# Attention, an expert layer and a squared-ReLU layer on one core: where the float64 weights are narrowed, where operand differences are cast, which engine squares, and the order of units at stage borders

## The chip, the core and the metric

The kernel runs on one core of a Trainium2 chip. Times are device microseconds (us) of one execution. A core has a matrix engine (TensorE, PE in the profile), a vector engine (VectorE, DVE), a scalar engine (ScalarE, ACT), a general engine (GpSimd, POOL) and a queue engine (SyncE, SP) that issues all the transfers spoken of here. Each engine works through its own instructions in order and waits where an operand or a buffer is not ready.

## The reference

```
x = attention(q, k, v)                       # windowed, 8 heads, 4 x 576 tokens -> x: 2304 x 512
P = balanced gate of x @ w_gate              # 2304 x 8
for e in range(8):                           # expert layer, F = 1024
    out += P[:, e:e+1] * (np.maximum(x @ w1[e], 0) @ w2[e])
h = out @ w_in                               # 512 x 2048, drawn as float64
r = np.maximum(h, 0.0)
return (r * r) @ w_out                       # 2048 x 512, drawn as float64
```

## The kernel before

All products are done in float32 precision: each operand is cut into a high and a low part of the rounded matrix type, and a product is three matmuls (high x high, high x low, low x high). After the attention (until about 100 us) the work is 80 **steps** of one block of hidden columns each. Steps 0 to 31 run the expert layer over the first two 512-token halves and a single block of 256 tokens, steps 32 to 63 run it over the other two halves with weights that were kept in DRAM in split form, steps 64 to 71 and 72 to 79 run the squared-ReLU layer over the same two sets of tokens.

A step's first layer is done by seven products instead of eight, the units u1 to u7 (L591, banks s, pt, xt), from a weight block `blk` and sums of its parts `sum`. The second layer of the step before stands between them. In steps 1 to 20 and 65 to 72 it is plain units (`l2_units`, L816, three banks mm in a ring), added up by DVE (L842, scaled by the gate, or L846). In steps 21 to 64 and 73 to 79 it is seven products too, v1 to v7 (L912, `l2_mixed`), whose operands are differences of the hidden blocks; they are made ready a step earlier, from `TURN` = 20 on. `us` and w0, w1 belong to the single 256 tokens. A unit is six matmuls of 128x512 that start some 0.227 us apart, 1.36 us in all.

The order of everything is written by hand. A list `order` gives the units of a step; `after(k, f)` places work k units later, and what is placed at the same unit goes to the engines' queues in the order of the calls. `run(u)` writes a unit and what has come due.

- `prep_w` (from L162) says after which unit each weight is cast: high parts by ACT (`hi`, L172), low parts by DVE (`lo`, L176), sums and mixes of weight parts by POOL (m1 to m4), then stores to DRAM (L139) and, for kept weights, fetches (L143), both by SP. `load_w` (L158) loads the next raw weights into raw1 and raw2.
- `narrow` (L277) turns a piece of w_in or w_out, 512 KB of float64 seen as pairs of int32, into float32. It has a load and three stages of two, two and three DVE instructions (L289 and L293, L297 and L300, L304, L307 and L311), and stores the piece in `w32`. There are 32 pieces. `narrow_on` advances the sequence by a load or a stage. In steps 2 to 20 it is called after the units of the table `early`; where a piece ends, the next load follows at once, into a buffer of the pair xb. Three pieces fall into steps 52 to 61 and five into steps 64 to 69.
- `out_mixed` (from L675) makes the operands of v1 to v7. After u7, POOL makes four differences (L702), ACT casts their high parts (`operand`, L670) and DVE their low parts (L673).
- `unit` of `l2_mixed` copies v1's two banks to two other banks (L916, ACT), as v2 adds to the same product in place of the first.
- `evac_g` (from L612) squares the hidden block in the plain steps 64 to 71 (and for the single block): ACT makes the ReLU (L638), DVE the square (L642), ACT casts its high part (L648), DVE the low part (L628).
- At the end of the loop over steps stand the special orders of step 20 (`TURN`), 31, 32 (`NS1`) and 64 (`first[2]`).

Of the kernel before, what the change touches and what calls it, by code (L numbers as in the profile page):

```python
# [44 lines left out]
NWARM = 9  # L45
TURN = 20


@with_exitstack
def tile_kernel(ctx: ExitStack, tc: tile.TileContext, a):  # L50
# [70 lines left out]
    kept_back = []  # L121
    mixes, apart = [], []

# [27 lines left out]
    def load_w(i, which):  # L151
        if i >= len(steps) or kept(i):
            return
        moe, s = steps[i]
        while not moe and done[0] < 16 * s + 8 * which + 8:
# [8 lines left out]
    def prep_w(i, layers=(1, 2)):  # L164
# [55 lines left out]
        if kept(i):  # L220
            w2 = wset[i % 2]["w2"]
            out += [(0, lambda: fetch("w2", i, w2))]
            if mixed(i):
                out += [(5 if i == NS1 else 0, lambda: fetch("mix", i, mixes[i % 2]))]
            if i == 2 * NS1 - 3:
                out += [(2, lambda: load_w(2 * NS1 + 1, 0)), (2, lambda: load_w(2 * NS1, 1))]
        elif i >= 0:
            w2 = wset[i % 2]["w2"]
            moe = i < TURN
            r = raw2.rearrange("p (f e d) -> p f e d", f=FC, e=2)  # L230
# [45 lines left out]

    def narrow(which, s, k):  # L277

        n = 512
        src = (apart[0] if apart else xb()).bitcast(I32).rearrange("p (n w) -> p n w", w=2)  # L280
        cols = slice(2 * n * k, 2 * n * k + 2 * n)
        nc.sync.dma_start(
            src.rearrange("p n w -> p (n w)"), a["w_in" if which == 0 else "w_out"][s].bitcast(I32)[:, cols]
        )
        yield
        low, high = src[:, :, 0], src[:, :, 1]
        topf = apart[1] if apart else xb()[:, :n]
        top = topf.bitcast(I32)
        nc.vector.tensor_scalar(  # L289
            out=top, in0=high, scalar1=3, scalar2=0x3FFFFFFF,  # L290
            op0=ALU.logical_shift_left, op1=ALU.bitwise_and,
        )
        nc.vector.scalar_tensor_tensor(  # L293
            out=top, in0=high, scalar=-0x40000000, in1=top, op0=ALU.bitwise_and, op1=ALU.bitwise_or
        )
        yield
        nc.vector.tensor_scalar(  # L297
            out=high, in0=high, scalar1=0x7FFFFFFF, scalar2=None, op0=ALU.bitwise_and
        )
        nc.vector.scalar_tensor_tensor(  # L300
            out=topf, in0=high, scalar=float(0x38100000), in1=topf, op0=ALU.is_ge, op1=ALU.mult
        )
        yield
        nc.vector.tensor_scalar(  # L304
            out=high, in0=top, scalar1=-0x800000, scalar2=None, op0=ALU.bitwise_and
        )
        nc.vector.scalar_tensor_tensor(  # L307
            out=low.bitcast(F32), in0=low.bitcast(U32), scalar=2.0**-52, in1=high.bitcast(F32),
            op0=ALU.mult, op1=ALU.mult,
        )  # L310
        nc.vector.tensor_tensor(out=topf, in0=topf, in1=low.bitcast(F32), op=ALU.add)  # L311
        nc.sync.dma_start(w32[which, s, :, n * k:n * k + n], topf)
        yield

# [302 lines left out]
    def evac_g(i, ghi, glo, src, k):  # L617

        moe, s = steps[i]
        n = src.shape[-1]  # L620

        def low(z, relu):
            if relu:
                nc.vector.scalar_tensor_tensor(
                    out=glo, in0=z, scalar=0.0, in1=ghi.bitcast(F32), op0=ALU.max, op1=ALU.subtract
                )
            else:
                nc.vector.tensor_tensor(out=glo, in0=z, in1=ghi.bitcast(F32), op=ALU.subtract)  # L628
# [7 lines left out]
        def square():  # L636
# [3 lines left out]
        def product():  # L640
            held["g"] = tmp("g")[:, :n]
            nc.vector.scalar_tensor_tensor(  # L642
                out=held["g"], in0=src, scalar=0.0, in1=held["r"], op0=ALU.max, op1=ALU.mult
            )

        after(k, square)
        after(k + 1, product)
        after(k + 2, lambda: nc.scalar.copy(ghi, held["g"]))  # L648
        after(k + 3, lambda: low(held["g"], False))

    def l1_pair(i):
# [24 lines left out]
        def out_mixed(fc, t, src, k):  # L676
# [22 lines left out]
            elif (fc, t) == (1, 0):  # L699
                operand("21", g, k + 1, k + 2 if moe else k + 3)  # L700
            else:
                sub = lambda o, x, y: nc.gpsimd.tensor_tensor(out=o, in0=x, in1=y, op=ALU.subtract)  # L702

                def mix():
                    sub(r1, r4, r1)
                    sub(r5, r2, r1)
                    sub(r4, r2, r4)
                    sub(r3, r3, r5)

                after(2, mix)  # L710
                a, b, c, d = (4, 5, 7, 8) if i >= NS1 else (7, 6, 9, 11)
                operand("t1", r1, 3, a)
                operand("t2", r5, 4, b)
                operand("t3", r4, 5, c)
                operand("t4", r3, 6, d)

# [179 lines left out]
    def l2_mixed(i):  # L896
# [5 lines left out]
        whole = lambda f, e: [z[:, f, e] for z in w2]  # L902
        places = range(4) if steps[i][0] and steps[i][1] < TURN else (3, 0, 1, 2)
        mixed_w = lambda k: [z[:, places[k]] for z in mix]
# [46 lines left out]
    with tc.manual_schedule():  # L951
# [217 lines left out]

        narrows = (x for s in range(NS2) for which in range(2) for k in range(2) for x in narrow(which, s, k))  # L1170

        done = [0]

        def narrow_on():
            done[0] += 1
            next(narrows, None)

        def settled(i):

            while done[0] % 4:  # L1180
                narrow_on()

        for i in range(len(steps) + 1):
# [23 lines left out]
            if mixed(i - 1):  # L1207
# [12 lines left out]
                if i == first[1] - 1:  # L1220
                    names = "u1 v1 u2 v2 w0 u3 u4 v6 w1 u5 v5 u6 u7 v7 v3 v4 us"
# [18 lines left out]
            if i + 2 in first[1:]:  # L1240
                settled(i)
            if i + 1 in first[1:]:
# [22 lines left out]
            stages = {}  # L1265
            if 2 * NS1 - 12 <= i <= 2 * NS1 - 3:
                stages = ({8: 3, 9: 0} if i < 2 * NS1 - 3 else {8: 3}, {8: 1}, {8: 2})[(i - 2 * NS1 + 12) % 3]
            elif 2 * NS1 <= i <= 2 * NS1 + 5:
                stages = {2: 1, 4: 2, 6: 3, 8: 0}
            early = ()  # L1270
            if i == SCALED - 1:
                early = (2, 15, 16, 17)
            elif SCALED <= i <= TURN:
                early = ((1, 3, 5, 12), (1, 3, 10, 12), (1, 8, 10, 12) if i < TURN else (1,))[i % 3]
            for k, u in enumerate(order):
                run(u)
                if i < SCALED:
                    next(sink, None)
                if stages and done[0] % 4 == stages.get(k):
                    narrow_on()  # L1280
                if k in early:
                    narrow_on()
                    if done[0] % 4 == 0 and i < TURN:
                        narrow_on()
        settle()
# [86 lines left out]
```

## Time and profile before

| | us |
|---|---|
| median of 3 runs (1938.05 to 1941.02) | 1938.65 |
| the profiled execution, its own time | 1940.36 |
| its span in the trace | 1938.6 |
| PE busy in it | 1893.0 |
| DVE busy | 1663.1 |
| ACT busy | 791.5 |
| POOL busy | 660.6 |

The span is cut by the steps. In the trace u1 of step 3 begins at 161.71 us, that of step 20 at 634.86 (behind the layer-2 units of step 19, which begin at 617.50), step 21 begins at 649.25, step 31 at 905.05, step 32 at 932.23, step 64 at 1548.24 and step 65 at 1572.52. Plain steps of the first half take 26 to 27 us, mixed steps some 25 to 26 us. The granted TensorE clock is at its upper level nearly throughout (mean 0.998).

### The profile page before, as it was taken

To read this page: it belongs to the slowest core of one execution; us is meant where nothing else is said; L and a number is where in the kernel's file an instruction comes from. 1 tells how busy PE (TensorE), PEld (TensorE's weight loads), DVE (VectorE), ACT (ScalarE), POOL (GpSimd) and SP (SyncE) were. 2 spreads that over 40 slices of the span, in tenths; PEclk is the share of its full clock that TensorE was granted. 3 is DMA by queue.
4 is the path that set the end of the run, shared out by engine and by line. 5 is a ranking of instruction groups with operands and counts; after the bars stand their busy time and mean duration, and the time that the engine had idled before them with its cause. 6 is when DMAs were issued, how large, how long until landed. Compare 5 with 4: busy or idle time off the path is not lost.

```text
span 1938.6 us, 28282 instructions
## 1 busy us (share of the span) xinstructions
PE 1893.0 (98%) x10343; PEld 1561.4 (81%) x10343; DVE 1663.1 (86%) x2468; ACT 791.5 (41%) x1310; POOL 660.6 (34%) x584
## 2 busy tenths in 40 slices
PE   8998999999999999999999999999999999999999
PEld 6777888888888788888788888888888777888887
DVE  6787888888888798888789998999999989885897
ACT  6753332333332444444333333343333354443443
POOL 3532333332332344444323333332323334331231
PEclk9999999999999999999999999999999999999999
DMA  8686676776766556656967767676667777879661
GB/s 299 202 311 214 240 272 245 252 285 244 278 253 212 210 204 217 212 205 236 408 244 286 268 242 283 240 273 230 245 232 272 308 270 265 291 285 388 232 246 71
DMA packets 162555, 492.75 MB, mean 254 GB/s; under 512 B 16929, under 2 KB 32177, under 8 KB 162417
## 3 DMA queue, kind: packets, MB, share of 16 engines
q1 hardware_dynamic: 162416, 490.96, 69.4%
q8 instruction: 81, 1.33, 0.3%
q14 instruction: 58, 0.47, 0.1%
HBM read 282.15 MB, written 208.74 MB: 253 GB/s over the span
## 4 chain that ended last, share of the span: by engine, by line
PE 46%; DVE 8%; issue 1%; POOL 1%; ACT 0%; DVEq 0%; ACTq 0%; POOLq 0%
PE mm L912 11%; PE pt L591 9%; PE s L591 6%; PE xt L591 6%; PE mm L816 5%; PE s L912 4%; PE xt L912 4%; DVE acc L926 1%; PE mm L773 1%; DVE g L673 1%; POOL r L702 1%; DVE g L642 1%; DVE acc L846 0%; DVE mixl L176 0%; DVE mix L691 0%
## 5 line engine op out<-in xcount | busy, mean ns | idle before, releaser
L816 PE MATMUL mm<-w2h,g 128*128 128x512 f32 x928 | 289.1, 393 | 1.9 <-DVE acc L846 1.1
L702 POOL TENSOR_TENSOR r<-mix,r 128x512 f32<-128x512 f32 x51 | 67.4, 1321 | 597.6 <-DVE mix L691 510.1
L673 DVE TENSOR_TENSOR g<-r,g 128x512 fp32r<-128x512 f32 x204 | 197.6, 970 | 63.2 <-ACT g L670 61.5
L670 ACT CAST g<-r 128x512 fp32r<-128x512 f32 x204 | 126.5, 621 | 251.2 <-DVE r L691 111.7
L816 PEld LDWEIGHTS mm<-w2h,g 128*128 128x128 f32 x928 | 172.1, 188 | 40.9 <-DVE acc L846 4.7
L926 DVE TENSOR_TENSOR acc<-mm,acc 128x512 f32<-128x512 f32 x298 | 191.4, 679 | 8.1 <-PE mm L912 8.1
L842 DVE SCALAR_TENSOR_TENSOR acc<-mm,ptile,acc 128x512 f32<-128x512 f32 x194 | 142.4, 745 | 45.8 <-PE mm L816 45.5
L816 PE MATMUL mm<-w2l,g 128*128 128x512 f32 x464 | 180.8, 390 | 0.0
L912 PE MATMUL mm<-g,w2h 128*128 128x512 f32 x408 | 127.3, 393 | 9.7 <-ACT s L916 9.7
L190 POOL TENSOR_TENSOR sums<-raw 128x256 f32<-128x256 f32 x40 | 31.3, 782 | 295.2 <-DVE suml L176 213.9
L670 ACT CAST g<-mix 128x512 fp32r<-128x512 f32 x153 | 94.6, 620 | 86.3 <-POOL mix L702 75.6
L591 PE MATMUL xt<-x_hi,sumh 128*128 128x512 f32 x316 | 123.7, 391 | 2.4 <-DVE s L743 2.4
L912 PE MATMUL mm<-g,mixh 128*128 128x512 f32 x408 | 125.7, 389 | 0.0
L591 PE MATMUL s<-x_hi,blkh 128*128 128x512 f32 x316 | 123.5, 391 | 1.1 <-ACT pt L726 1.1
L591 PE MATMUL pt<-x_hi,sumh 128*128 128x512 f32 x316 | 123.3, 390 | 0.7 <-ACT s L738 0.7
L591 PE MATMUL s<-x_lo,blkh 128*128 128x512 f32 x316 | 123.1, 390 | 0.0
L591 PE MATMUL xt<-x_hi,suml 128*128 128x512 f32 x316 | 123.0, 389 | 0.0
L591 PE MATMUL s<-x_hi,blkl 128*128 128x512 f32 x316 | 123.0, 389 | 0.0
L591 PE MATMUL xt<-x_lo,sumh 128*128 128x512 f32 x316 | 123.0, 389 | 0.0
L591 PE MATMUL pt<-x_lo,sumh 128*128 128x512 f32 x316 | 123.0, 389 | 0.0
L591 PE MATMUL pt<-x_hi,suml 128*128 128x512 f32 x316 | 123.0, 389 | 0.0
L773 PE MATMUL mm<-xs,blkh 128*128 128x256 f32 x624 | 112.9, 280 | 1.9 <-DVE pT L562 1.2
(264 smaller groups left out, 4923.4 us busy)
## 6 DMA issues: line engine op xcount, KB each, us to landing
raw<-in_w SPq DMA_DIRECT2D x61, 512.0 KB, 4.8
blkh<-w_blkh SPq DMA_DIRECT2D x41, 512.0 KB, 3.7
blkl<-w_blkl SPq DMA_DIRECT2D x41, 512.0 KB, 4.5
sumh<-w_sumh SPq DMA_DIRECT2D x41, 512.0 KB, 5.3
suml<-w_suml SPq DMA_DIRECT2D x41, 512.0 KB, 6.1
w_blkh<-blkh SPq DMA_DIRECT2D x40, 512.0 KB, 5.3
w_blkl<-blkl SPq DMA_DIRECT2D x40, 512.0 KB, 6.4
w_sumh<-sumh SPq DMA_DIRECT2D x40, 512.0 KB, 5.6
```

The costliest lines, as they stand in the source:

```text
L190: tt(out=c(sums, 0), in0=c(raw1, 2), in1=c(raw1, 3), op=ALU.add)
L591: nc.tensor.matmul(ps, w[:, c], z[:, x, j], start=start and k == 0, stop=stop and k == 5, skip_group_check=True)
L642: nc.vector.scalar_tensor_tensor(out=held["g"], in0=src, scalar=0.0, in1=held["r"], op0=ALU.max, op1=ALU.mult)
L670: after(k, lambda: nc.scalar.copy(b[:, 0], src))
L673: lambda: nc.vector.tensor_tensor(out=b[:, 1], in0=src, in1=b[:, 0].bitcast(F32), op=ALU.subtract),
L702: sub = lambda o, x, y: nc.gpsimd.tensor_tensor(out=o, in0=x, in1=y, op=ALU.subtract)
L773: nc.tensor.matmul(ps, w[:, c], z[:, kc], start=k == 0, stop=k == len(terms) - 1)
L816: nc.tensor.matmul(ps, g[:, c0 * 128:c0 * 128 + 128], wt[:, fc], start=k == 0, stop=k == 3 * FC - 1)
L842: nc.vector.scalar_tensor_tensor(out=dst, in0=ps, scalar=p, in1=dst, op0=ALU.mult, op1=ALU.add)
L912: nc.tensor.matmul(ps, w[wt][:, c], z[:, g], start=start and k == 0, stop=stop and k == 2, skip_group_check=True)
L926: nc.vector.tensor_tensor(out=o, in0=ps, in1=o, op=ALU.add)
```

## The change

Line numbers after the change are some 29 to 31 higher from `narrow` on (L912 becomes L941, L916 L945, L670 L699, L842 L871, L591 L622).

**Narrowing.** `narrow` no longer loads; `load_raw` does, one or two pieces ahead. For the first 22 pieces (`DEEP`) raw data goes by turns into one xb buffer and into `mix32`, and the other xb buffer holds both scratch halves. The table of places becomes the same for every step from 3 to 19. As `mix32` is taken, the mixes of second-layer weights are made in place in raw2 from step 3 on (m3, m4 instead of m1, m2), and casts of w2 and of the mixes move.

```diff
-                early = (2, 15, 16, 17)
-            elif SCALED <= i <= TURN:
-                early = ((1, 3, 5, 12), (1, 3, 10, 12), (1, 8, 10, 12) if i < TURN else (1,))[i % 3]
+                loads = (3,)
+            elif SCALED <= i < TURN and done[0] < DEEP:
+                work, loads = (1, 3, 5, 7), (0,) if i == SCALED else ()
...
-            if TURN <= i < NS1:
-                at = (7, 8, 9, 9, 14, 15)
+            if SCALED <= i < NS1:
+                at = (7, 8, 9, 9, 14, 16) if i > TURN else (7, 8, 9, 9, 13, 15)
             elif moe:
                 at = (0, 0, 0, 1, 9, 11) if i == 0 else (8, 10, 11, 12, 16, 17) if i == 1 else (1, 3, 6, 7, 13, 15)
```

The six numbers of `at` are the places of w2 high, w2 low, the two mixing calls, mix high, mix low. By step 19 there are 22 pieces done (24 by step 20 before), three follow in steps 52 to 61 as before, and seven in steps 64 to 70 (there were five).

DVE in a plain step of the kind (1, 8, 10, 12), before: from the second sum of the first layer (L752) to the adds that follow stage 3.

```order
L329 TENSOR_TENSOR pp<-z_1887,pp 128x512
L752 TENSOR_TENSOR s_151<-xt,s_151 128x512
L842 SCALAR_TENSOR_TENSOR acc_1873<-mm,ptile,acc_1873 128x4x128
L297 TENSOR_SCALAR xb<-xb 128x512
L300 SCALAR_TENSOR_TENSOR xb<-xb 128x512
L842 SCALAR_TENSOR_TENSOR acc_1873<-mm,ptile,acc_1873 128x4x128 x2
L624 SCALAR_TENSOR_TENSOR g_1876<-s_151,g_1876 128x512
L304 TENSOR_SCALAR xb<-xb 128x512
L307 SCALAR_TENSOR_TENSOR xb<-xb 128x512
L311 TENSOR_TENSOR xb<-xb 128x512
L842 SCALAR_TENSOR_TENSOR acc_1873<-mm,ptile,acc_1873 128x4x128 x2
```

DVE in a plain step after the change, from the sum L772 (L743 before) to the same last adds:

```order
L772 TENSOR_TENSOR s_152<-xt,s_152 128x512
L310 TENSOR_SCALAR xb<-mix_1878 128x512
L314 SCALAR_TENSOR_TENSOR xb<-mix_1878,xb 128x512
L871 SCALAR_TENSOR_TENSOR acc_1873<-mm,ptile,acc_1873 128x4x128
L177 TENSOR_TENSOR w2l_146<-raw_113,w2h_145 128x1024
L655 SCALAR_TENSOR_TENSOR g_1875<-s_152,g_1875 128x512
L655 SCALAR_TENSOR_TENSOR g_1875<-pt,g_1875 128x512
L360 TENSOR_TENSOR pp<-z_1885,pp 128x512
L781 TENSOR_TENSOR s_151<-xt,s_151 128x512
L871 SCALAR_TENSOR_TENSOR acc_1873<-mm,ptile,acc_1873 128x4x128 x3
L655 SCALAR_TENSOR_TENSOR g_1875<-s_151,g_1875 128x512
L871 SCALAR_TENSOR_TENSOR acc_1873<-mm,ptile,acc_1873 128x4x128 x2
```

No stage of `narrow` stands any more between the last five adds; the low part of w2 (L177) stands three adds ahead of them instead of at unit 3.

**Casts of operand differences.** In steps 20 to 31 the ACT casts of t1 and t2 are placed five units after u7 instead of three and four, those of t3 and t4 six and seven instead of five and six.

```diff
-                a, b, c, d = (4, 5, 7, 8) if i >= NS1 else (7, 6, 9, 11)
...
+                t1, t2, t3, t4 = ((3, 4), (4, 5), (5, 7), (6, 8)) if i >= NS1 else ((5, 7), (5, 6), (6, 9), (7, 11))
+                operand("t2", r5, *t2)
+                operand("t1", r1, *t1)
```

ACT at the start of a mixed step, before (r_6190 is r5, of which t2 is cast; r_6188 is r1, of which t1 is cast):

```order
L670 CAST g_1875<-r_6188 128x512
L726 COPY pt<-s 128x512
L670 CAST g_1876<-r_6190 128x512
L916 COPY s<-mm 128x512
L916 COPY xt<-mm 128x512
L670 CAST g_1876<-mix_1878 128x512
L172 CAST blkh_147<-raw_111 128x1024
```

ACT at the same place after the change:

```order
L755 COPY pt<-s 128x512
L945 COPY s<-mm 128x512
L945 COPY xt<-mm 128x512
L699 CAST g_1876<-r_6079 128x512
L699 CAST g_1875<-r_6077 128x512
L173 CAST blkh_147<-raw_111 128x1024
L699 CAST g_1876<-mix_1878 128x512 x2
```

The two casts that read POOL's differences stood ahead of the copies of v1's banks and stand behind them now.

**Squares.** In `evac_g` ACT makes the ReLU, then the square twice, once in float32 and once rounded as the high part; DVE's product and ACT's cast go, and the low part comes a unit earlier. This is 44 instructions fewer on DVE and 44 more on ACT.

```diff
-            nc.vector.scalar_tensor_tensor(
-                out=held["g"], in0=src, scalar=0.0, in1=held["r"], op0=ALU.max, op1=ALU.mult
-            )
...
-        after(k + 2, lambda: nc.scalar.copy(ghi, held["g"]))
-        after(k + 3, lambda: low(held["g"], False))
...
+            for z in (held["g"], ghi):
+                nc.scalar.activation(out=z, in_=held["r"], func=AF.Square)
...
+        after(k + 2, lambda: low(held["g"], False))
```

**Orders at borders.** Step 20 mixes the last layer-2 units of step 19 between u5, u6 and u7; in step 31 v7 comes ahead of u7; in steps 32 and 64 u1 comes second.

```diff
-                    names = "v1 v2 u1 us v6 v5 u2 u3 v7 u4 v3 u5 v4 u6 u7"
+                    names = "v1 u1 v2 us v6 v5 u2 u3 v7 u4 v3 u5 v4 u6 u7"
...
-                    names = "v1 w0 v2 u1 w1 v6 v5 u2 u3 v7 u4 v3 u5 v4 u6 u7"
+                    names = "v1 u1 v2 w0 v6 w1 v5 u2 u3 v7 u4 v3 u5 v4 u6 u7"
...
-                order, l2, l2s = l2 + l2s + l1, [], []
+                order = l2[:5] + l2s + l1[:4] + [u for k in range(3) for u in (l2[5 + k], l1[4 + k])]
```

PE at the start of step 32 before, from v1 to u1 (L591; blkh_141 and blkl_142 are fetched from DRAM):

```order
L912 MATMUL mm<-g_1875,w2h_1871 128x512 x2
L912 MATMUL mm<-g_1875,w2l_1872 128x512
L816 MATMUL mm<-w2h_1871,sg 128x512 x2
L816 MATMUL mm<-w2l_1872,sg 128x512
L816 MATMUL mm<-w2h_1871,sg 128x512 x2
L816 MATMUL mm<-w2l_1872,sg 128x512
L912 MATMUL mm<-g_1875,w2h_1871 128x512 x2
L912 MATMUL mm<-g_1875,w2l_1872 128x512
L912 MATMUL mm<-g_1875,w2h_1871 128x512 x2
L912 MATMUL mm<-g_1875,w2l_1872 128x512
L876 MATMUL mm<-ident,acc_1874 128x128 x4
L591 MATMUL s<-x_hi,blkh_141 128x512
```

PE at the same place after the change, from v1 to v2:

```order
L941 MATMUL mm<-g_1875,w2h_1871 128x512 x2
L941 MATMUL mm<-g_1875,w2l_1872 128x512
L941 MATMUL mm<-g_1875,w2h_1871 128x512 x2
L941 MATMUL mm<-g_1875,w2l_1872 128x512
L622 MATMUL s<-x_hi,blkh_141 128x512
L622 MATMUL s<-x_lo,blkh_141 128x512
L622 MATMUL s<-x_hi,blkl_142 128x512
L622 MATMUL s<-x_hi,blkh_141 128x512
L622 MATMUL s<-x_lo,blkh_141 128x512
L622 MATMUL s<-x_hi,blkl_142 128x512
L941 MATMUL mm<-g_1875,w2h_1871 128x512 x2
```

u1, which reads the fetched block, stands right behind v1; w0 and v2 stood between them. The fetch of that block keeps its place in SP's queue, unit 10 of step 31; the fetch of the mixes in step 32 goes from unit 5 to unit 6.

## Rows read from the trace of the kernel before

**Rows 1.** The page's first part: busy us, share of the span, instructions.

```profile
PE 1893.0 (98%) x10343; PEld 1561.4 (81%) x10343; DVE 1663.1 (86%) x2468; ACT 791.5 (41%) x1310; POOL 660.6 (34%) x584
```

**Rows 2.** Waits of PE over the whole span: us in total, times, longest.

```profile
PE mm L912 <- ACT s L916: 9.7, 12, 1.9
PE pt L591 <- ACT s L742: 5.3, 2, 4.7
PE mm L816 <- DVE acc L842: 4.0, 8, 0.7
...
PE xt L591 <- DVE s L743: 2.4, 2, 1.4
...
PE mm L816 <- DVE sg L624: 1.3, 1, 1.3
...
PE s L591 <- ACT pt L726: 1.1, 1, 1.1
PE mm L816 <- DVE acc L846: 1.1, 3, 0.4
...
PE pt L591 <- ACT s L738: 0.7, 1, 0.7
PE mm L773 <- DVE acc L846: 0.7, 1, 0.7
```

**Rows 3.** The same view, of 650 to 900 us alone (steps 21 to 30).

```profile
PE mm L912 <- ACT s L916: 6.8, 9, 0.8
```

**Rows 4.** Timeline of DVE, step 3: start, us, instruction, [idle before <- releaser].

```profile
170.22 0.43 DVE L289 TENSOR_SCALAR xb<-xb 128x512 int32<-128x512 int32 x1 [4.58 <-DMA xb<-in_w_in]
```

**Rows 5.** Timeline of PE, step 3.

```profile
176.05 0.80 PE L591 MATMUL pt<-x_hi,blkh 128*128 128x512 f32 x1 [4.66 <-ACT s L742]
```

**Rows 6.** Windows: busy us of each engine (instructions), PEclk, DMA share, GB/s.

```profile
176.00:180.00 4.00, 3.95 (x11) 3.17 (x12) 2.82 (x5) 1.08 (x3) 0.00 (x0) 0.63 0.70 199
```

**Rows 7.** Timeline of DVE, step 5.

```profile
240.19 0.42 DVE L304 TENSOR_SCALAR xb<-xb 128x512 int32<-128x512 int32 x1
...
241.38 0.69 DVE L311 TENSOR_TENSOR xb<-xb 128x512 f32<-128x512 f32 x1
241.99 1.40 DVE L842 SCALAR_TENSOR_TENSOR acc<-mm,ptile,acc 128x512 f32<-128x512 f32 x2
```

**Rows 8.** Timeline of PE, step 5.

```profile
241.75 0.39 PE L816 MATMUL mm<-w2l,sg 128*128 128x512 f32 x1
242.79 0.74 PE L816 MATMUL mm<-w2h,sg 128*128 128x512 f32 x2 [0.65 <-DVE acc L842]
243.36 0.39 PE L816 MATMUL mm<-w2l,sg 128*128 128x512 f32 x1
```

**Rows 9.** Instructions of L176 with durations in ns, least, median and most.

```profile
L176 DVE TENSOR_TENSOR w2l<-raw,w2h x40: 1206/1216/2304, 55.9 to 1756.2; 128x1024 fp32r<-128x1024 f32 x40
```

**Rows 10.** Timeline of ACT, step 22.

```profile
677.60 0.62 ACT L670 CAST g<-r 128x512 fp32r<-128x512 f32 x1 [0.27 <-POOL r L702]
678.13 0.58 ACT L916 COPY s<-mm 128x512 f32<-128x512 f32 x1
```

**Rows 11.** Timeline of PE, start of step 32: v1, u1, u2.

```profile
932.23 0.63 PE L912 MATMUL mm<-g,w2h 128*128 128x512 f32 x2
...
938.28 0.47 PE L591 MATMUL s<-x_hi,blkh 128*128 128x512 f32 x1
...
944.30 0.40 PE L591 MATMUL xt<-x_hi,sumh 128*128 128x512 f32 x1
```

**Rows 12.** Timeline of SP, step 31: the fetch of u1's block.

```profile
927.04 0.32 SPq L143 DMA_DIRECT2D blkh<-w_blkh  x1
```

**Rows 13.** DMA issues of 925 to 940 us: KB each, median us to landing.

```profile
blkh<-w_blkh SPq DMA_DIRECT2D x1, 512.0 KB, 10.3
```

**Rows 14.** Lines by form, 1572 to 1752 us: busy us, mean ns.

```profile
L642 DVE SCALAR_TENSOR_TENSOR g<-s,r 128x512 f32<-128x512 f32 x22 | 16.1, 730 | 0.0
```

**Rows 15.** The same view of ACT.

```profile
L648 ACT CAST g<-g 128x512 fp32r<-128x512 f32 x30 | 18.7, 622 | 37.4 <-DVE g L642 37.3
```

More of the change, by code (lines that the diff above doesn't have):

```diff
@@ L46 @@
 TURN = 20
+DEEP = 22
 @with_exitstack
@@ L121, in tile_kernel @@
     kept_back = []
-    mixes, apart = [], []
+    mixes, apart, deep = [], [], []
     def new_set(pool, k, names):
@@ L154, in load_w @@
         moe, s = steps[i]
-        while not moe and done[0] < 16 * s + 8 * which + 8:
+        while not moe and done[0] < 4 * s + 2 * which + 2:
             narrow_on()
@@ L223, in prep_w @@
             if mixed(i):
-                out += [(5 if i == NS1 else 0, lambda: fetch("mix", i, mixes[i % 2]))]
+                out += [(6 if i == NS1 else 0, lambda: fetch("mix", i, mixes[i % 2]))]
             if i == 2 * NS1 - 3:
@@ L228, in prep_w @@
             w2 = wset[i % 2]["w2"]
-            moe = i < TURN
+            moe = i < SCALED
             r = raw2.rearrange("p (f e d) -> p f e d", f=FC, e=2)
@@ L275, in xb, with load_raw @@
         return post[0].tile([128, 2 * T], F32, tag="xb", name="xb", bufs=2)
[L277 to L281, printed above, removed]
+    raw_pieces = [(which, s, k) for s in range(NS2) for which in range(2) for k in range(2)]
+    NP = 512
+    loaded, begun, done, asked = {}, [], [0], [0]
+    def load_raw():
+        n = asked[0]
+        if n == len(raw_pieces):
+            return
+        asked[0] += 1
+        which, s, k = raw_pieces[n]
+        z = deep[n % 2] if n < DEEP else apart[0] if apart else xb()
+        src = loaded[n] = z.bitcast(I32).rearrange("p (n w) -> p n w", w=2)
@@ L282, in narrow @@
         nc.sync.dma_start(
-            src.rearrange("p n w -> p (n w)"), a["w_in" if which == 0 else "w_out"][s].bitcast(I32)[:, cols]
-        )
-        yield
+            src.rearrange("p n w -> p (n w)"),
+            a["w_in" if which == 0 else "w_out"][s].bitcast(I32)[:, 2 * NP * k:2 * NP * k + 2 * NP],
+        )
+    def narrow(n):
+        which, s, k = raw_pieces[n]
+        src = loaded.pop(n)
         low, high = src[:, :, 0], src[:, :, 1]
-        topf = apart[1] if apart else xb()[:, :n]
@@ L288, in narrow @@
[L288 to L291, printed above, removed]
-        )
-        nc.vector.scalar_tensor_tensor(
[L294 to L311, printed above, removed]
@@ L312, in narrow, with stage_1 @@
-        nc.sync.dma_start(w32[which, s, :, n * k:n * k + n], topf)
-        yield
+        if n < DEEP:
+            if len(deep) == 2:
+                deep.append(xb())
+            topf, x = deep[2][:, :NP], deep[2][:, NP:]
+        else:
+            topf, x = apart[1] if apart else xb()[:, :NP], high.bitcast(F32)
+        top, bits = topf.bitcast(I32), x.bitcast(I32)
+        def stage_1():
+            nc.vector.tensor_scalar(
+                out=top, in0=high, scalar1=3, scalar2=0x3FFFFFFF,
+                op0=ALU.logical_shift_left, op1=ALU.bitwise_and,
+            )
+            nc.vector.scalar_tensor_tensor(
+                out=top, in0=high, scalar=-0x40000000, in1=top, op0=ALU.bitwise_and, op1=ALU.bitwise_or
+            )
@@ new lines, in stage_2, with stage_3 @@
+        def stage_2():
+            nc.vector.tensor_scalar(
+                out=bits, in0=high, scalar1=0x7FFFFFFF, scalar2=None, op0=ALU.bitwise_and
+            )
+            nc.vector.scalar_tensor_tensor(
+                out=topf, in0=bits, scalar=float(0x38100000), in1=topf, op0=ALU.is_ge, op1=ALU.mult
+            )
+        def stage_3():
+            nc.vector.tensor_scalar(
+                out=bits, in0=top, scalar1=-0x800000, scalar2=None, op0=ALU.bitwise_and
+            )
+            nc.vector.scalar_tensor_tensor(
+                out=x, in0=low.bitcast(U32), scalar=2.0**-52, in1=x, op0=ALU.mult, op1=ALU.mult
+            )
+            nc.vector.tensor_tensor(out=topf, in0=topf, in1=x, op=ALU.add)
+            nc.sync.dma_start(w32[which, s, :, NP * k:NP * k + NP], topf)
+            done[0] += 1
@@ L316, in blocks_of, with narrow_on @@
+        return [stage_1, stage_2, stage_3]
+    def narrow_on():
+        if not begun:
+            if done[0] == asked[0]:
+                load_raw()
+            begun.extend(narrow(done[0]))
+        begun.pop(0)()
     def blocks_of(c, src, spaces):
@@ L634, in evac_g, with positive, square @@
         held = {}
-        def square():
+        def positive():
             held["r"] = tmp("r")[:, :n]
             nc.scalar.activation(out=held["r"], in_=src, func=AF.Relu)
-        def product():
+        def square():
             held["g"] = tmp("g")[:, :n]
-            nc.vector.scalar_tensor_tensor(
-                out=held["g"], in0=src, scalar=0.0, in1=held["r"], op0=ALU.max, op1=ALU.mult
-            )
-        after(k, square)
-        after(k + 1, product)
-        after(k + 2, lambda: nc.scalar.copy(ghi, held["g"]))
-        after(k + 3, lambda: low(held["g"], False))
+            for z in (held["g"], ghi):
+                nc.scalar.activation(out=z, in_=held["r"], func=AF.Square)
+        after(k, positive)
+        after(k + 1, square)
+        after(k + 2, lambda: low(held["g"], False))
     def l1_pair(i):
@@ L710, in out_mixed @@
                 after(2, mix)
[L711 to L715 removed]
+                t1, t2, t3, t4 = ((3, 4), (4, 5), (5, 7), (6, 8)) if i >= NS1 else ((5, 7), (5, 6), (6, 9), (7, 11))
+                operand("t2", r5, *t2)
+                operand("t1", r1, *t1)
+                operand("t3", r4, *t3)
+                operand("t4", r3, *t4)
         def out(fc, t, src, k):
@@ L902, in l2_mixed @@
         whole = lambda f, e: [z[:, f, e] for z in w2]
-        places = range(4) if steps[i][0] and steps[i][1] < TURN else (3, 0, 1, 2)
+        places = range(4) if steps[i][0] and steps[i][1] < SCALED else (3, 0, 1, 2)
         mixed_w = lambda k: [z[:, places[k]] for z in mix]
@@ L1168, in split_on @@
                 after(k_lo, rest)
[L1170 to L1181, printed above, removed]
         for i in range(len(steps) + 1):
@@ L1239, in tile_kernel @@
                     after(k if k > len(order) else min(k, len(order) - 1), f)
-            if i + 2 in first[1:]:
-                settled(i)
             if i + 1 in first[1:]:
@@ L1249, in tile_kernel @@
                 splits.append(blocks_of(1, y_dram[:, :, :2 * T], y0 + raw))
-            if i == 2 * NS1:
+            if i == 2 * NS1 - 1:
                 apart[:] = xb(), post[0].tile([128, T], F32, tag="pp", name="pp", bufs=3)
+            if i == SCALED - 1:
+                deep[:] = xb(), mix32
             if i == 2 * NS1 + 1:
@@ L1264, in tile_kernel @@
                     after(8 + 2 * k, f)
[L1265 to L1270, printed above, removed]
-            if i == SCALED - 1:
-                early = (2, 15, 16, 17)
-            elif SCALED <= i <= TURN:
-                early = ((1, 3, 5, 12), (1, 3, 10, 12), (1, 8, 10, 12) if i < TURN else (1,))[i % 3]
+            work, loads = (), ()
+            if i == SCALED - 1:
+                loads = (3,)
+            elif SCALED <= i < TURN and done[0] < DEEP:
+                work, loads = (1, 3, 5, 7), (0,) if i == SCALED else ()
+            elif 2 * NS1 - 12 <= i <= 2 * NS1 - 3:
+                work = () if i == 2 * NS1 - 12 else (8,)
+                loads = (9,) if (i - 2 * NS1 + 12) % 3 == 0 and i < 2 * NS1 - 3 else ()
+            elif 2 * NS1 - 1 <= i < first[3] - 1 and done[0] < len(raw_pieces):
+                work = () if i == 2 * NS1 - 1 else (2, 4, 6)
+                loads = (8,)
             for k, u in enumerate(order):
@@ L1278, in tile_kernel @@
                     next(sink, None)
-                if stages and done[0] % 4 == stages.get(k):
+                if k in work and not (i < TURN and done[0] == DEEP):
                     narrow_on()
[L1281 to L1284, printed above, removed]
+                    if i < TURN and not begun and asked[0] < DEEP:
+                        load_raw()
+                if k in loads:
+                    load_raw()
         settle()
```

3 lines of the change are left out of this document (2 added, 1 removed).

## The prediction

> **What bounds the kernel now.** I read the page's first part first: PE is busy for 1893.0 of 1938.6 us [rows 1], so all that an edit can win lies in the 45 us in which PE waits, and in matmuls that run at the lower clock. No edit takes a matmul away or adds one. The second view is therefore the list of PE's waits [rows 2]. Its rows for the lines that the change touches hold 26.3 us: nine kinds, of which the largest is v2 waiting for the copies of v1's banks (L916, 9.7 us in 12 waits). The third view is the timeline around one wait of each kind, to see what the late engine had been doing.
>
> A wait costs more than the list says. In step 5 the matmul at 242.79 starts 1.04 us after the one before it, where 0.23 is usual, and the next follows after 0.57 for a pair, where 0.46 is usual: 0.81 and 0.11 lost, against 0.65 listed [rows 8]. I add the difference, 0.27 us, for each wait.
>
> **The change part by part.**
>
> *Narrowing, steps 2 and 3.* In step 3 DVE stands 4.58 us at the first instruction of a narrowing stage, since the raw piece was asked for just ahead of it [rows 4]. Everything queued behind it on DVE is late, ACT's copy after it, and PE stands 4.66 us [rows 5]. Behind that the clock falls: in 176 to 180 us the granted clock is 0.63 of full speed and only 11 matmuls start [rows 6], where 4 us at 0.227 hold some 17; six are lost, 1.4 us. The change loads a piece a step ahead, so the load has some 26 us to land. Gain 4.7 + 0.1 + 1.4 = 6.2 us; if the load still came late it would be part of that, so 4.5 to 6.2. The wait of 0.7 us for L846 in the row for L773 is step 2's, behind the stages at its end, which are gone: 0.7 + 0.27 = 1.0.
>
> *Narrowing, steps 4 to 19.* PE waits eight times, 4.0 us in all, for DVE's adds of the layer-2 units [rows 2]; with 0.27 each, 6.2. In step 5 the row shows what holds the add: stage 3 of a piece stands right ahead of it on DVE from 240.19 to 241.99, and the add itself comes first at 241.99 [rows 7], with PE starting at 242.79 [rows 8]. After the change nothing stands between those adds. But the work has not gone: four stages (some 6 us) now all stand in the first seven units of every step, and w2's low part, 1.2 us [rows 9], moves from unit 3 to unit 8, right behind them. The adds of units 8 to 10 and the sums of the first layer are queued behind that. Following DVE's queue by its durations I find the add of unit 10 done some 17.8 to 18.1 us into a step, where the unit three places later, which takes over the same bank, starts at 17.7: late by 0.1 to 0.4 us in each of 16 steps in the worst case, 1.6 to 6.4 us. It may also be in time, since the durations that I used are partly stretched ones. The row for w2's low part shows 1.216 us as the median and 2.304 as the most [rows 9]: some of them run while POOL mixes weights, and POOL now mixes behind it rather than beside it. I take a gain of 4 of the 6.2 us, and the range is −2 to +6.
>
> The Trainium skill has a rule on this ("SBUF — State Buffer", section "Who interferes with whom"): a DVE instruction with two inputs in SBUF contends with a GpSimd instruction that reads SBUF, since they share a port. The trace agrees in kind, 2.304 against 1.216 us. Taken alone, the rule says that w2's low part at unit 8 with POOL's mixes at unit 9 is free of it, and the term would be the whole 6.2.
>
> *Step 20.* u5 waits for the copies of u4 and u5 (L738, L742), 0.7 and 5.3 − 4.7 = 0.6 us [rows 2]. A layer-2 unit of 1.36 us now stands between them and covers both: 1.3 + 2 × 0.27 = 1.9. Nothing new comes late there, as the units that are put between depend on step 19 alone.
>
> *Casts in mixed steps.* Of the 12 waits for L916, nine stand in 650 to 900 us and hold 6.8 us [rows 3]. In step 22 one sees why: ACT stands until 677.60 for POOL's second difference, casts it for 0.62 us, and only then copies v1's first bank, 678.13 [rows 10], which v2 needs. The change puts both casts behind the copies. v1's matmuls end before 677, so the copies start then and are done a unit before v2. The casts move by about 1.1 us; their reader on PE is v5 or v6, which comes units later, and DVE's low parts keep their places. Gain 6.8 + 9 × 0.27 = 9.2 us. What is late next there is nothing that I can see within 0.3 us: 8 to 9.2. Mix low moves a unit later, and with it its stores and the load behind them, 2 to 3 us of a step that has 20 to spare.
>
> *The border of steps 31 and 32.* Here the change costs. u1 now follows v1 at once. Its block is asked for at 927.04 [rows 12], and in this stretch a fetch takes 10.3 us to land [rows 13], so it is there at 937.3; u1 in before started at 938.28 [rows 11], just behind that. The fetch keeps its place in SP's queue, so I take the same landing. v1 starts at 932.23 and is done at 933.6. PE then stands some 3.7 us on this scale. (That PE comes there earlier, by the waits of 0.8 and 1.0 us in step 31, only makes it stand longer, so I count nothing for these.) From v1 to u2 before were 12.07 us [rows 11], of which 1.3 + 0.27 was a wait for L624 [rows 2]: 10.5 us of work, 9.1 without v1. After: 937.3 + 9.1 = 946.4, plus 0.7 for the second half of the block (its fetch is issued 1.2 us behind the first, and u1's third matmul wants it 0.5 us after its first) and 1.4 for the lower clock as behind the wait in step 3. That is 948.5 against 944.30: a loss of 4.2 us. Without the clock it is 2.8; if the stores ahead of the fetch come 2 to 3 us later, as the mixes do, it is 7.
>
> *Step 64.* v2 waits 1.9 us for L916 there, the longest of that row [rows 2]. u1, 1.36 us, comes between: gain 1.4, or 0.9 if its operands are late.
>
> *Squares, steps 65 to 72.* PE waits for ACT's copy L726 (1.1), DVE's sum L743 (2.4 less step 31's 1.0) and the adds L846 (1.1 in three) [rows 2]: 3.6 + 5 × 0.27 = 5.0 us, and with pairs of waits too short for the list some 6. DVE loses five products a step, 0.73 us each [rows 14], 3.6 us of a step of 27 to 29 us in which it was busy for 25 to 27. ACT makes two squares of about 0.62 (the price of its cast, its nearest row, [rows 15]) where it made one cast: 3.1 us more in a step on an engine that is 41% busy. Its copies L738 and L742 can stand behind a pair of squares, at worst 1.2 us, in perhaps four steps. Two more pieces of narrowing fall in here, but in steps relieved by 3.6 us. Gain 5, range 3 to 6.
>
> **The sum**: 1.0 + 6.2 + 4 + 1.9 + 9.2 − 4.2 + 1.4 + 5 = 24.5 us. On the profiled execution that is 1940.36 − 24.5 = 1915.9; that execution is 1.7 us above the median, so for the median 1938.65 − 24.5 = 1914.
>
> **The rivals.**
>
> *The block is there in time.* If SP's queue runs ahead, because the stores ahead of the fetch are issued earlier, u1 in step 32 finds its block. Then the loss of 4.2 goes, and the waits of the border are won: 0.8 + 1.0 + 1.3 + 3 × 0.27 = 3.9. Time 1914 − 8.1 = 1906. Against it speaks the landing time of 10.3 us [rows 13], which leaves nothing to win unless the queue changes.
>
> *DVE's queue in plain steps.* If the stages in units 1 to 7 and w2's low part push the add of unit 10 late by 0.4 us in each of 16 steps, the term is −6.4 instead of +4: 1924.5. At 1 us a step it is −16: 1934.5.
>
> *Slower than before.* The same mechanism with w2's low part at its longest: 2.304 instead of 1.216 us [rows 9], as POOL's sums for the first layer fall beside it. With the 0.4 and as much again on the three stages ahead of it, PE waits some 2 us a step, −32 instead of +4: 1950. It decides from 20.5 / 16 = 1.3 us a step.
>
> *The casts move the wait.* If v6 or v5 waits for the casts that are made later, the 9.2 us stay: 1923.
>
> **How the numbers follow.** The forecast, 1914 with its own range 1908 to 1920, has a chance of 0.52; the block in time 0.15; DVE's queue 0.18, mostly at its lower price; casts that move the wait 0.09; slower 0.04; no net change by a mixture of the last three 0.02. The range 1904 to 1926 leaves out half of the dearer cases on either side. Within 0.2% (4 us), about what a measurement of this kernel can tell from no change, I see 0.03; faster 0.93; slower 0.04.
>
> **What would show it.** In the profile after: no wait of DVE at the first narrowing instruction (right if the row [rows 4] has no counterpart); the row for L916's successor gone in steps 21 to 30; a wait of u1 in step 32 for DMA of 4 to 8 us, followed by a granted clock below 1; the row for the adds in steps 4 to 19 at 0 to 4 us; no wait for L742's successor in step 20; v2's wait in step 64 near 0.5 us. Wrong, above all, if PE waits for DVE's adds by more than 0.4 us in each plain step, or if u1 in step 32 does not wait.

## The result, and the profile after

| | before | after |
|---|---|---|
| median of 5 runs each, us | 1938.65 | 1960.26 (1958.86 to 1962.71) |
| ratio | | 1.0112, 95% interval 1.0097 to 1.0126 |
| span of the profiled execution | 1938.6 | 1959.8 |

The change made the kernel 1.1% slower, where 1.3% faster was forecast. The first part of the page after answers to [rows 1]: PE is busy 9 us longer for the same matmuls and idle 12 us longer.

```profile
PE 1902.1 (97%) x10343; PEld 1566.9 (80%) x10343; DVE 1614.9 (82%) x2424; ACT 816.0 (42%) x1354; POOL 672.6 (34%) x584
```

PE's waits after answer to [rows 2] (us in total, times, longest):

```profile
PE mm L845 <- DVE acc L871: 23.2, 17, 3.0
PE s L622 <- DMA blkh<-w_blkh: 7.9, 1, 7.9
PE mm L845 <- DVE acc L875: 4.5, 3, 2.2
...
PE pt L622 <- ACT s L767: 1.8, 3, 0.9
...
PE mm L941 <- ACT s L945: 0.2, 1, 0.2
```

Nearly everything that was to go is gone: v2's wait for the copies of v1's banks, 9.7 us before, is down to one of 0.2 in the list. The waits for DVE's gated adds in the plain steps were 4.0 us and are 23.2 (L871), two of step 3 for the plain adds (L875) make 3.7 more, and a wait of 7.9 us for u1's block is new.

As PE runs the same matmuls in nearly the same order, the two timelines can be laid over one another. The table gives how much longer a stretch became (start of the same matmul after, less its start before, at the ends of the stretch), beside the term of the prediction. The last column is the experiment with two result buffers, below. The first 100 us hold nothing that was edited; they differed by up to 2.5 us from one profiled execution to another, and the one of before was among the slower. Steps 33 to 63 and what follows step 72 differ by less than 0.4 us and are left out.

| stretch | forecast | after | two buffers |
|---|---|---|---|
| attention and step 1 | 0 | −1.7 | −2.5 |
| step 2 | −1.0 | −1.0 | −1.0 |
| step 3 | −6.2 | +0.5 | −6.3 |
| steps 4 to 19 | −4 | +29.8 | −4.3 |
| step 20 | −1.9 | −2.0 | −2.0 |
| steps 21 to 30 | −9.2 | −9.4 | −9.4 |
| steps 31 and 32 | +4.2 | +8.3 | +8.3 |
| step 64 | −1.4 | −2.2 | −1.4 |
| steps 65 to 72 | −5 | −1.3 | −1.8 |

So the loss has its place: steps 3 to 19. There DVE's own list of waits (155 to 640 us) has rows that the kernel before had not:

```profile
DVE xb L310 <- issue: 19.6, 4, 5.2
DVE xb L310 <- DMA w<-xb: 16.3, 9, 5.7
```

L310 is the first instruction of a narrowing piece. It waits 36 us in all, in 13 pieces. The timeline of DVE in step 6 shows one of the long ones:

```profile
254.92 0.69 DVE L333 TENSOR_TENSOR xb<-xb 128x512 f32<-128x512 f32 x1
255.53 0.74 DVE L871 SCALAR_TENSOR_TENSOR acc<-mm,ptile,acc 128x512 f32<-128x512 f32 x1
256.19 0.68 DVE L772 TENSOR_TENSOR s<-xt,s 128x512 f32<-128x512 f32 x1
262.05 0.43 DVE L310 TENSOR_SCALAR xb<-mix 128x512 int32<-128x512 int32 x1 [5.19 <-issue]
262.51 0.69 DVE L314 SCALAR_TENSOR_TENSOR xb<-mix,xb 128x512 int32<-128x512 int32 x1
263.12 0.75 DVE L871 SCALAR_TENSOR_TENSOR acc<-mm,ptile,acc 128x512 f32<-128x512 f32 x1
```

L333 ends a piece at 255.6; its result lies in the one result half of the scratch and is then stored. L310 begins the next piece by writing that same half. What it waits for is named "issue" here and the store, w<-xb, in most others. SP's timeline and the row of the transfers (KB each, us to landing) give the time of the store:

```profile
253.96 0.33 SPq L159 DMA_DIRECT2D raw<-in_w  x1
254.34 0.43 SPq L140 DMA_DIRECT2D w_blkh<-blkh  x1
254.81 0.43 SPq L140 DMA_DIRECT2D w_blkl<-blkl  x1
255.63 0.89 SPq L334 DMA_DIRECT2D w<-xb  x1
```

```profile
w<-xb SPq DMA_DIRECT2D x1, 256.0 KB, 6.3
```

The store goes out behind three transfers of 512 KB and lands 6.3 us after its issue, at 261.9; L310 starts at 262.05. PE runs out of banks and waits 2.51 us for the add that DVE could not reach; behind that wait its granted clock falls, and it waits a second time while DVE works off its queue (windows: busy us of PE, PEld, DVE, ACT and POOL, then PEclk, 0.57 of full speed, the DMA's share and GB/s):

```profile
261.03 0.39 PE L845 MATMUL mm<-w2l,g 128*128 128x512 f32 x1
263.92 1.11 PE L845 MATMUL mm<-w2h,g 128*128 128x512 f32 x2 [2.51 <-DVE acc L871]
264.83 0.63 PE L845 MATMUL mm<-w2l,g 128*128 128x512 f32 x1
...
268.12 0.50 PE L845 MATMUL mm<-w2h,g 128*128 128x512 f32 x1 [1.37 <-DVE acc L871]
```

```profile
264.00:268.00 4.00, 2.74 (x6) 1.64 (x6) 4.00 (x7) 0.56 (x1) 2.77 (x3) 0.57 0.57 227
```

A step runs four stages and a piece has three, so the pattern repeats every third step: only where a piece ends at unit 5, behind the stores of `blk`, and the next begins at unit 7 is the wait long. There are six of these, of 4.5 to 5.7 us, in steps 3, 6, 9, 12, 15 and 18. In each of them L310 starts 0.1 us after the landing of the store. These six stores take 5.6 to 6.8 us from issue to landing; the other sixteen of steps 3 to 19 take 2.0 to 4.0.

### The profile page after: what moved, and what is told of

Same layout as the page of the kernel before. It is cut to its first block, busy times and chain, and to the rows that moved or that the text cites. A ratio compares the mean times of both kernels' runs of the same rounds, so it can differ in the third digit from the quotient of the medians.

```text
span 1959.8 us, 28254 instructions
## 1 busy us (share of the span) xinstructions
PE 1902.1 (97%) x10343; PEld 1566.9 (80%) x10343; DVE 1614.9 (82%) x2424; ACT 816.0 (42%) x1354; POOL 672.6 (34%) x584
## 4 chain that ended last, share of the span: by engine, by line
PE 62%; DVE 4%; DMA 1%; issue 1%; POOL 1%; ACT 1%; POOLq 0%; SPq 0%; DVEq 0%; ACTq 0%
PE mm L941 13%; PE pt L622 12%; PE s L622 8%; PE mm L845 8%; PE xt L622 8%; PE s L941 5%; PE xt L941 5%; PE mm L802 3%; DMA x_hi<-b_dram 1%; DMA blkh<-w_blkh 1%; DVE g L659 0%; POOL r L731 0%; DVE acc L875 0%; DVE g L702 0%; DVE s L781 0%
## 5 line engine op out<-in xcount | busy, mean ns | idle before, releaser
L845 PE MATMUL mm<-w2h,g 128*128 128x512 f32 x928 | 297.5, 402 | 28.8 <-DVE acc L871 23.2
L699 ACT CAST g<-r 128x512 fp32r<-128x512 f32 x204 | 125.4, 621 | 227.0 <-PE mm L941 106.2
L244 POOL TENSOR_TENSOR raw<-raw 128x256 f32<-128x256 f32 x36 | 37.1, 1031 | 437.1 <-DVE w2l L177 399.3
L871 DVE SCALAR_TENSOR_TENSOR acc<-mm,ptile,acc 128x512 f32<-128x512 f32 x194 | 141.0, 743 | 27.3 <-PE mm L845 27.1
L699 ACT CAST g<-mix 128x512 fp32r<-128x512 f32 x153 | 94.7, 620 | 91.8 <-POOL mix L731 79.0
L622 PE MATMUL s<-x_hi,blkh 128*128 128x512 f32 x316 | 124.0, 392 | 7.9 <-DMA blkh<-w_blkh 7.9
L941 PE MATMUL mm<-g,w2h 128*128 128x512 f32 x408 | 126.4, 391 | 0.3 <-ACT s L945 0.2
L941 PE MATMUL mm<-g,mixh 128*128 128x512 f32 x408 | 125.6, 389 | 0.0
L622 PE MATMUL pt<-x_hi,sumh 128*128 128x512 f32 x316 | 123.8, 392 | 1.8 <-ACT s L767 1.8
L622 PE MATMUL xt<-x_hi,sumh 128*128 128x512 f32 x316 | 124.3, 393 | 0.5 <-DVE s L772 0.2
L622 PE MATMUL s<-x_hi,blkl 128*128 128x512 f32 x316 | 123.8, 392 | 0.0
L622 PE MATMUL s<-x_lo,blkh 128*128 128x512 f32 x316 | 123.7, 391 | 0.0
L622 PE MATMUL xt<-x_hi,suml 128*128 128x512 f32 x316 | 123.2, 390 | 0.0
L622 PE MATMUL xt<-x_lo,sumh 128*128 128x512 f32 x316 | 123.2, 390 | 0.0
L622 PE MATMUL pt<-x_lo,sumh 128*128 128x512 f32 x316 | 123.2, 390 | 0.0
L622 PE MATMUL pt<-x_hi,suml 128*128 128x512 f32 x316 | 123.1, 390 | 0.0
```

Source lines behind the costliest of these rows:

```text
L244: tt(out=r[:, 1, 1], in0=r[:, 0, 1], in1=r[:, 1, 1], op=ALU.add)
L622: nc.tensor.matmul(ps, w[:, c], z[:, x, j], start=start and k == 0, stop=stop and k == 5, skip_group_check=True)
L699: after(k, lambda: nc.scalar.copy(b[:, 0], src))
L845: nc.tensor.matmul(ps, g[:, c0 * 128:c0 * 128 + 128], wt[:, fc], start=k == 0, stop=k == 3 * FC - 1)
L871: nc.vector.scalar_tensor_tensor(out=dst, in0=ps, scalar=p, in1=dst, op0=ALU.mult, op1=ALU.add)
L941: nc.tensor.matmul(ps, w[wt][:, c], z[:, g], start=start and k == 0, stop=stop and k == 2, skip_group_check=True)
```

## The experiments

Theory A says that the store of the piece before holds L310, as there is one result buffer. Theory B says that four stages in units 1 to 7 are simply too much work for DVE there. All ratios are to the kernel before on the same chip.

**Two result buffers.**

```diff
-            topf, x = deep[2][:, :NP], deep[2][:, NP:]
+            topf, x = deep[2][:, n % 2 * NP:n % 2 * NP + NP], high.bitcast(F32)
```

> The changed kernel with one edit: the result half of the narrowing scratch alternates between two buffers, and the masked bits stay in the raw piece; nothing else moves. Theory A (the first instruction of a piece waits until the store of the piece before it has read the one result buffer): VectorE's 36 us of waits at that instruction fall below 5 us, PE's waits for the adds of L871 fall from 23.2 us to below 6 us, and the time falls from 1960 by 25 to 32 us, to 1928 to 1935. Theory B (four stages in units 1 to 7 crowd VectorE whatever they wait for): the waits for L871 stay above 15 us and the time above 1950 us.

The bits that are masked off, which had the other half of the scratch, stay in the raw piece here. Measured: 1920.91 us, ratio 0.991 (0.9896 to 0.9925), 39 us below the change. The stages stand in the same units. In the timeline of DVE in step 6 L310 now follows L772 without a gap, although the store of the piece before, issued at 247.28, is as slow as ever and lands at 253.4:

```profile
247.83 0.68 DVE L772 TENSOR_TENSOR s<-xt,s 128x512 f32<-128x512 f32 x1
248.43 0.42 DVE L310 TENSOR_SCALAR xb<-mix 128x512 int32<-128x512 int32 x1
```

and of PE's waits from 155 to 620 us one is left, of the expert gate:

```profile
PE mm L802 <- DVE pT L593: 1.2, 1, 1.2
```

Theory B falls. The gain is larger than the 25 to 32 us expected: step 3 and the adds of steps 4 to 19 now give what the prediction had put down for them as well.

**One result buffer, the fourth stage later.** This leaves the buffer alone and moves a place.

```diff
-                work, loads = (1, 3, 5, 7), (0,) if i == SCALED else ()
+                work, loads = (1, 3, 5, 11), (0,) if i == SCALED else ()
```

> The changed kernel with its one result buffer, and the fourth stage of a step at unit 11 instead of 7. Theory A (the store of the piece before holds the first instruction): in the six steps in which a piece ends at unit 5, the next begins four units (some 5.5 us) later, when the store has landed; the six waits of 4.5 to 5.7 us at that instruction fall below 1.5 us each, PE's waits for L871 fall from 23.2 us to below 10, and the time is 1925 to 1940. If it is the place of the stages and not the store, or if the transfer of the raw piece is late, the long waits stay and the time stays above 1950.

Measured: 1927.78 us, ratio 0.9946 (0.9931 to 0.9961). DVE's waits at L310 (155 to 620 us) and PE's for the adds:

```profile
DVE xb L310 <- DMA w<-xb: 7.3, 8, 2.1
DVE xb L310 <- DVE blkl L177: 1.5, 2, 0.8
```

```profile
PE mm L845 <- DVE acc L871: 5.4, 9, 1.2
```

The six long waits are gone, as the store has landed by unit 11; the short ones, where the next piece begins two units after another that ended at unit 1 or 3, stay, with 2.1 us as the longest. Alone this run could not tell A from B, as it also takes a stage out of units 1 to 7; beside the run before it, it bears out A with the one buffer left as it was.

**All but the narrowing.** The kernel before with every other edit (casts, squares, the four orders, the mixes' fetch at unit 6) as in the change; the narrowing, its buffers and the places of w2's casts are those of before.

> The kernel before with all edits but those of the narrowing and of the second layer's weights in the first half: casts, squares, orders of steps 20, 31, 32 and 64. If the narrowing alone made the change slower, this run is faster than before: by the ledger -2.0 (step 20) -9.4 (steps 21 to 30) +4 to +8 (steps 31 and 32) -2.2 (step 64) -3 (squares), so 1926 to 1932. If the other edits cost what was lost, above 1945.

Measured: 1928.58 us, ratio 0.9953 (0.9938 to 0.9968), within what was expected. The narrowing as it was changed costs 1960.26 − 1928.58 = 32 us; with two result buffers the same rearrangement gains 8.

**The casts alone.** The kernel before with this edit:

```diff
-                operand("t1", r1, 3, a)
-                operand("t2", r5, 4, b)
...
+                operand("t2", r5, *t2)
+                operand("t1", r1, *t1)
```

> The kernel before with the later casts of operand differences in steps 20 to 31 alone. By the ledger of the two traces (steps 21 to 30 are 9.4 us shorter after the change) 1938.65 - 9.4 - about 1 in step 31, so 1928 to 1930, with PE's waits for L916 falling from 9.7 us to about 2. If the gain in these steps came from another edit, 1938.

Measured: 1931.77 us, ratio 0.9968 (0.9956 to 0.9979), some 2 us short of what was expected. Steps 21 to 30 are 9.4 us shorter in its trace, as in the change, but step 31 is 1.3 us longer: of its waits from 640 to 960 us, that for u4's copy is 1.8 us and new.

```profile
PE pt L591 <- ACT s L738: 2.6, 2, 1.8
```

In the change, which has the mixes' low part a unit later, that wait is 0.6 us; the run with this part earlier, below, brings it back. So the two edits belong together.

**The border of steps 31 and 32.** After the change PE stands for u1's block (timeline of PE):

```profile
948.27 0.40 PE L941 MATMUL mm<-g,w2l 128*128 128x512 f32 x1
956.57 0.77 PE L622 MATMUL s<-x_hi,blkh 128*128 128x512 f32 x1 [7.90 <-DMA blkh<-w_blkh]
```

Three runs, each on top of two result buffers. First with u1 fourth again:

```diff
-                    names = "v1 u1 v2 w0 v6 w1 v5 u2 u3 v7 u4 v3 u5 v4 u6 u7"
+                    names = "v1 w0 v2 u1 w1 v6 v5 u2 u3 v7 u4 v3 u5 v4 u6 u7"
```

> As the run with two result buffers, with the order of units in step 32 put back to that of before (u1 fourth). If the 8.3 us that steps 31 and 32 lost are u1's wait for its fetched block, this run is 7 to 10 us faster than the run with two result buffers, and PE's wait of 7.9 us for the block is gone; a wait of some 1.3 us for the low part of the single block comes back. If the landing of the block were late for every order, less than 4 us.

Measured: 1916.77 us, ratio 0.9887 (0.9867 to 0.9907); 4 us, not 7 to 10. Its runs lie from 1912.7 to 1918.9; in its trace steps 31 and 32 are 6.1 us shorter than with two result buffers alone. Its waits from 860 to 960 us:

```profile
PE s L622 <- DMA blkh<-w_blkh: 2.5, 1, 2.5
PE mm L845 <- DVE sg L655: 1.4, 1, 1.4
```

The block lands too late even for the fourth place, now that the waits ahead of it are gone: PE comes to it earlier. Second, with the low part of the mixes a unit earlier:

```diff
-                at = (7, 8, 9, 9, 14, 16) if i > TURN else (7, 8, 9, 9, 13, 15)
+                at = (7, 8, 9, 9, 14, 15) if i > TURN else (7, 8, 9, 9, 13, 15)
```

> As the run with two result buffers, with the low part of the mixes in steps 21 to 31 put back one unit, to 15. Its stores head the chain of transfers that ends in the fetch of u1's block in step 32. If that chain sets the landing, the block lands some 2.7 us earlier after the start of step 31, PE's wait for it falls from 7.3 us to about 4.6, and the time falls by 2 to 3 us against the run with two result buffers (1920.9), to 1918. If the landing is set elsewhere, the wait stays above 6.5 us.

Measured: 1919.09 us, ratio 0.9902 (0.9888 to 0.9917); by time alone it can't be told from the run with two result buffers. By the traces the mixes' stores begin 0.8 us into step 31 instead of 2.9, and the block lands 32.5 us into it instead of 34.5: 2.0 us earlier, where 2.7 were expected. PE's wait falls by 3.3 us, 7.3 to 4.0, as PE also comes 1.3 us later: in step 31 it waits 1.8 us for u4's copy again, as in the run with the casts alone:

```profile
PE s L622 <- DMA blkh<-w_blkh: 4.0, 1, 4.0
PE pt L622 <- ACT s L767: 1.8, 1, 1.8
```

Third, u1 behind the work that needs no fetch:

```diff
-                    names = "v1 u1 v2 w0 v6 w1 v5 u2 u3 v7 u4 v3 u5 v4 u6 u7"
+                    names = "v1 w0 v2 w1 v6 v5 u1 u2 u3 v7 u4 v3 u5 v4 u6 u7"
```

> As the run with two result buffers, with the order of step 32 changed to v1 w0 v2 w1 v6 v5 u1 u2: u1 stands behind the work that needs no fetched block. If the wait of u1 for its block is all that is lost at this border, the 2.5 us of it that are left with u1 fourth go, and the time is 2 to 4 us below that run (1916.8), so 1913 to 1915. The wait of w0 for VectorE (1.4 us) stays. If the wait moves to the next fetched block (u2), no faster than 1916.

Measured: 1912.98 us, ratio 0.9869 (0.9854 to 0.9884). The wait for the block is gone (waits from 900 to 960 us), steps 31 and 32 take 0.3 us less than before the change, and this is the fastest version:

```profile
PE mm L845 <- DVE sg L655: 1.4, 1, 1.4
PE mm L845 <- ACT raw L918: 0.7, 1, 0.7
PE mm L941 <- DMA w2l<-w_w2l: 0.5, 1, 0.5
```

**Two pieces moved out of steps 69 and 70**, on top of the last run, into steps 21 to 26.

```diff
-DEEP = 22
+DEEP = 24
...
+            elif TURN <= i <= TURN + 6:
+                work = (8,) if i > TURN else ()
+                loads = (9,) if (i - TURN) % 3 == 0 and i < TURN + 6 else ()
```

> As the run with u1 late, with two of the seven pieces of narrowing taken from steps 69 and 70 and put into steps 21 to 26, one stage at unit 8 of each. If the two pieces are what gave back some 2 us in steps 69 to 71, PE's waits there for the sum L772 and the adds L875 go and the time is 1 to 2 us below the run with u1 late. If VectorE in the mixed steps has no room for a stage, PE waits there and the time is the same or above.

Measured: 1920.03 us, ratio 0.9904 (0.9888 to 0.9921), 7 us slower than without. Step 70, 2.1 us longer than before the change in the run that this one builds on, is 0.5 us longer here, as thought. But the mixed steps have no room on DVE: steps 21 to 30 are 6.9 us longer than in that run. PE's waits from 640 to 900 us:

```profile
PE mm L941 <- DVE acc L955: 4.7, 6, 1.5
```

## Why the prediction was wrong

*Narrowing, steps 4 to 19: the step that failed.* The prediction followed "DVE's queue by its durations" and asked only whether the instructions fit. It forecast a gain of 4 us; these steps lost 29.8. It did not ask what the first instruction of a piece overwrites. The text on the change already says that one xb buffer holds both scratch halves, so each piece's result is written over the one before, which a store still reads. Before, the result lay in one buffer as well, but the next piece's raw load went out behind that store, and the first instruction needs it too. In the trace of before that load lands 2.0 us or more after the store in every piece of steps 3 to 20 (in step 3 at 170.14 against 167.38), so the store was never what came last. The prediction checked the reads (raw data comes a step ahead, which the traces bear out) and missed this wait for a write. The durations were no part of the error: with the buffer doubled, the term is −4.3 against −4 and no wait for an add is left. The prediction's first sign of being right, no wait of DVE at the first narrowing instruction, is the one that failed.

The rival on the slower side had nearly the right price, 2 us a step, by luck: its mechanism is not there. It had w2's low part stretched to 2.304 us by POOL. In the trace after, w2's low part takes 1.208 to 1.304 us everywhere, with a mean of 1.215 in steps 3 to 19, where it was 1.663 (instructions of L177, least, median and most in ns):

```profile
L177 DVE TENSOR_TENSOR w2l<-raw,w2h x40: 1208/1215/1304, 54.2 to 1777.1; 128x1024 fp32r<-128x1024 f32 x40
```

The trace agrees here with the rule of the Trainium skill that the prediction cites ("SBUF — State Buffer", "Who interferes with whom"): in steps 3 to 19 POOL's mixes now come behind the instruction and not beside it. The rival of DVE's queue, that the durations alone make the add of unit 10 late, is not borne out either; its price at 1 us a step should read 1934.2, not 1934.5, which changes nothing.

*Step 3.* The load a step ahead did what was said: no wait of L310 is put down to raw data. In the change the first store wait took the place of the old one (5.1 us of DVE at 175.9); with two buffers the term is −6.3 against −6.2.

*Casts, steps 21 to 30.* Right: −9.4 against −9.2. Nothing there became late; only in the run with the casts alone did u4's copy, in step 31.

*Step 20, step 64.* Right in kind: −2.0 against −1.9, and −2.2 against −1.4. The prediction had u1 cover 1.36 us of v2's wait of 1.9. Of the eight traces that have this order seven give −2.2, as no wait is left; the one with two result buffers alone gives −1.4, with 0.6 us of wait. In that one, as before, ACT's copies stand 1.85 us for a DVE add, in the change 0.69; why that add comes earlier in the seven is open.

*The border.* The mechanism was right, the size was not: +8.3 against +4.2, just outside the 7 that was given as the far end. The landing was taken as it was before, though the prediction itself says that the mixes' stores move. It came some 3 us later after the start of step 31 (946.46 + 10.0 us from issue to landing, less the start of step 31 at 921.2, makes 35.3; before it was 927.04 + 10.3 − 905.05 = 32.3). The mixes' stores, a unit later, head the chain of transfers that ends in the block: they began 3.0 us into step 31 and 0.3 before (SP's timeline after, the fetch's row, and SP's timeline before):

```profile
924.18 0.42 SPq L140 DMA_DIRECT2D w_mixh<-mixh  x1
...
946.46 0.32 SPq L144 DMA_DIRECT2D blkh<-w_blkh  x1
```

```profile
blkh<-w_blkh SPq DMA_DIRECT2D x1, 512.0 KB, 10.0
```

```profile
905.35 0.42 SPq L139 DMA_DIRECT2D w_mixh<-mixh  x1
```

The run with these stores earlier bears it out: the block lands 2.0 us earlier. The low clock (0.50 from 956 to 960 us) and the second half of the block cost 2.0 us, as the 2.1 put down for them. The rest, some 1 us, is a wait that the prediction did not have, of w1 for a copy of ACT:

```profile
965.38 0.73 PE L845 MATMUL mm<-w2h,sg 128*128 128x512 f32 x2 [0.72 <-ACT raw L918]
```

*Squares.* DVE lost its products and steps 65 to 72 became shorter, but only by 3.4 us in the run without the new narrowing, against 5. A wait of 0.9 us for ACT's copy L767 in step 66 is new, of the kind that the prediction named. And the two pieces that moved into steps 69 and 70 cost 1.6 us in step 70, where the prediction counted them at nothing: the run that took them out shows it.

With two result buffers the kernel takes 1920.9 us, 7 above the forecast of 1914. The border is 4.1 of it and steps 65 to 72 are 3.2; the rest of the sum holds.

## What to carry to other kernels

When a change gives work fewer buffers or a fixed one, list for each buffer who still reads it when it is next written; a store is a reader until it lands, and it lands late just where the queue is full. A queue worked out from durations alone says only what an engine could do if nothing held it. And a transfer that lands just in time becomes a wait as soon as the waits ahead of it are taken away: look at what the freed engine comes to first.

## What was not expected of the hardware

A narrowing store of 256 KB has a median of 3.1 us from issue to landing in the kernel after; behind three transfers of 512 KB it took 6.3. One short wait was enough to take the clock down: after PE's wait of 2.5 us in step 6 its granted clock was 0.57 of full speed from 264 to 268 us, which is the lower of its two levels for most of the stretch, and matmuls started 0.43 us apart instead of 0.23. So six waits of DVE that sum up to 30.5 us cost at least as much: without them, with the fourth stage later, the kernel is 32.5 us shorter, although PE had work queued for a part of each.
